# Linear attention and a gated FFN in one kernel: the order of work in the opening and in block 1

## The chip, the cores and the metric

The kernel runs on one core of one Trainium2 chip. The metric is device time in microseconds (us). The time before is the median of 11 runs. One more execution was recorded by the hardware profiler, and all durations of single instructions come from that one.

## What is computed

Inputs are q, k and v (batch 8, 8 heads, 576 positions, head dimension 64), the FFN's weights and a norm weight, all float32. The reference, cut to what matters:

```python
def phi(x, c, s):                       # c, s: cos and sin of the position
    r = np.maximum(x, 0.0)
    return np.concatenate([r * c, r * s], axis=-1)
q_p, k_p = phi(q, cos_w, sin_w), phi(k, cos_w, sin_w)
kv = np.einsum('bhsf,bhsd->bhfd', k_p, v)
z = np.sum(k_p, axis=2)
num = np.einsum('bhsf,bhfd->bhsd', q_p, kv)
den = np.einsum('bhsf,bhf->bhs', q_p, z)[..., None] + 1e-06
attn = num / den                        # then x = attn as (4608 tokens, 512)
rms = np.sqrt(np.mean(x * x, axis=-1, keepdims=True) + 1e-06)
xn = x / rms * rms_g
g = xn @ w_gate                         # 512 -> 1536
silu = g * (1.0 / (1.0 + np.exp(-g)))
out = (silu * (xn @ w_val)) @ w_out     # 1536 -> 512
```

## The kernel before

**Tiling.** Attention goes by batch. A batch has four chunks of 128 positions per head plus a tail of 64; two tails share a tile. The FFN goes by blocks of 512 tokens: block b holds the four chunks of batch b, and block 8 holds the tails of all eight. A block has 12 gval steps and then four out tiles (three and two halves for block 8). Gval step n computes 128 of the 1536 hidden columns for 512 tokens: four matmuls into a psG bank, four into a psV bank (gval_mm, L444), a Silu on ScalarE (ACT) out of psG (L453), and a multiply on VectorE (DVE) out of psV into hT (L459). An out tile is 12 matmuls of 512 columns into one bank (out_mm, L464), a copy to osb (out_store, L272 on ACT, L274 on DVE) and a store.

**Attention of a batch.** k_phi and q_phi make the feature map, one half on DVE (L215), one on ACT (L213). v_cast (L276) turns v to bf16 in two halves, LOW and HIGH (four heads each), v_cast_tail the tail on GpSimd. kvz_pe (L300) makes kv and z for eight heads, in psA, and kvz_evac copies them out. q is transposed, by DMA (q_tr_dma, L255) or, for batches 0 and 1, on TensorE (q_tr_pe, L263, and a copy, q_tr_evac). nd_pe (L328) makes numerator and denominator of a chunk in psA, nd_post (L378, L381, L382, DVE) divides, x_sq (L393, ACT) sums squares, GpSimd takes the power -0.5 (L398), x_norm (L405, DVE) scales, and x is transposed by DMA (x_tr_dma, L424) or on TensorE (x_tr_pe, L430, with a copy, x_tr_evac).

**Banks.** Of the eight PSUM banks psA has two, psG two, psV two. The last two are psO in the opening and psC, for the out tiles, afterwards. psA serves kvz, nd and some transposes in turn, so each waits until the one before has been read.

**Order.** The schedule is written out by hand: every engine works through its instructions in program order, and semaphores make it wait for data and for buffers to come free. Nothing is reordered by a planner.

- *Opening* (L488 to L626): batch 0's attention and, as its x chunks come, block 0's gval steps 0 to 5 in column pieces (open_ffn, L569, and open_h, L580 and L581) in three pairs of banks. Filler matmuls on a tile of zeros (L484) lie where TensorE would wait.
- *Block 0's steps 6 to 11*, with batch 1's phi work in between.
- *Out tiles of block 0* (L739 to L788): four tiles at once, in psC[0], psC[1], psG[0], psG[1], with batch 1's attention in between. At the end come four out_store, the first quarter of block 1's gval and the last x transposes of batch 1.
- *Blocks 1 to 8*: the loop at L808. A table of slots (at, L638; run, L641) hangs work of the next batch on a step: "pe" ahead of the step's matmuls, "pre" after the matmuls and ahead of Silu and multiply (or of out_store), "post" after them. Steps 12 to 15 are the out tiles. For batch 2 (`late`) all of it hangs on block 1: phi of k on steps 0 to 2, q on 2 to 4, v casts on 4 and 5, kvz on 6, nd on 7, 9, 11 and 12. For later batches k and v are done in the block before. (1,6) below means block 1, step 6.

**Queues.** Loads, stores and DMA transposes are issued from the SP queue, in program order; weights are issued from GpSimd's. The first slice of wo waits for k of batch 1, which waits for the third slice of w_gate. Batch 2 is loaded whole from L758 to L760; batch 3 in pieces of two heads hung on block 1's steps.

Of the kernel before, what the change touches and what calls it, by code (L numbers as in the profile page):

```python
# [22 lines left out]
def kernel(  # L23
# [18 lines left out]
    NNT = DFF // P  # L42
# [11 lines left out]
    psA = ps.tile([P, 2, 512], FP32, name="psA")  # L54
    psG = [ps.tile([P, 512], FP32, name=f"psG{i}") for i in range(2)]
    psV = [ps.tile([P, 512], FP32, name=f"psV{i}") for i in range(2)]
# [4 lines left out]
    psO = [ps_open.tile([P, 512], FP32, name=f"psO{i}") for i in range(2)]  # L61

    V, A, G = nc.vector, nc.scalar, nc.gpsimd
    LOW, HIGH = (0, 4), (4, 8)
# [143 lines left out]
    def view4(t, heads):  # L208
        return t[:, heads[0] : heads[1], :].rearrange("p h (j d) -> p h j d", d=D)

    def phi(eng, out_ap, in_ap, scale):
        if eng is nc.scalar:
            nc.scalar.activation(out=out_ap, in_=in_ap, func=AF.Relu, scale=scale)  # L213
        else:
            eng.tensor_scalar(  # L215
                out=out_ap, in0=in_ap, scalar1=scale, scalar2=0.0, op0=ALU.mult, op1=ALU.max
            )

    def k_phi(eng, b, c, part, heads=(0, 8)):

        o = slice(0, D) if part == 0 else slice(D, F)
        f = cos_of if part == 0 else sin_of
        if c < 4:
            if b not in kp_main:
                kp_main[b] = one.tile([P, 4, H, F], BF16, name="kpm", tag="kpm")
            src = view4(raw[("k", b)], heads)[:, :, c, :]
            phi(eng, kp_main[b][:, c, heads[0] : heads[1], o], src, f(c))
        else:
            phi(eng, kpt[b % 2][:, :, o], raw[("kt", b)][:, :, :], f(4))
# [35 lines left out]
    def q_tr_evac(eng, b, c, bank, heads=(0, 8)):  # L265
        h0, h1 = heads if c < 4 else (0, 4)
        dst = bank.bitcast(BF16).rearrange("p (h s) -> p h s", s=P)
        copy(eng, q_dst(b, c)[:, h0:h1, :], dst[:, h0:h1, :])
# [157 lines left out]
    def x_tr_pe(b, j, bank):  # L426
        xn = xn_of[(b, j)]
        dst = bank.bitcast(BF16).rearrange("p (t s) -> p t s", s=P)
        for t in range(NDT):
            nc.tensor.transpose(dst[:, t, :], xn[:, t * P : (t + 1) * P], ident[:, :])  # L430

    def x_tr_evac(eng, b, j, bank, part=(0, 4)):
        dst = bank.bitcast(BF16).rearrange("p (t s) -> p t s", s=P)
        copy(eng, x_dst(b, j)[:, part[0] : part[1], :], dst[:, part[0] : part[1], :])
# [5 lines left out]
    def gval_mm(blk, n, bank, cols=(0, TB), parts=((psG, wg), (psV, wv))):  # L440
        x = xnT[blk]
        for pst, w in parts:
            for t in range(NDT):
                nc.tensor.matmul(  # L444
                    pst[bank][:, cols[0] : cols[1]],
                    lhsT=w[:, t, n * P : (n + 1) * P],
                    rhs=x[:, t, cols[0] : cols[1]],
                    start=(t == 0), stop=(t == NDT - 1),
                )
# [13 lines left out]
    def out_mm(blk, j, n, bank):  # L463
        nc.tensor.matmul(  # L464
            bank, lhsT=hTs[blk][:, n, j * P : (j + 1) * P], rhs=wo[:, n, :],
            start=(n == 0), stop=(n == NNT - 1),
        )

    def out_store(eng, blk, j, bank):
        osb = four.tile([P, DM], FP32, name="osb", tag="osb")  # L470
        copy(eng, osb[:, :], bank)
        if blk < 8:
            rows = out[blk * S : blk * S + 512, :].rearrange("(p j) m -> p j m", j=4)
            nc.sync.dma_start(out=rows[:, j, :], in_=osb[:, :])  # L474
        else:
            for i in range(2):
                r0 = (2 * j + i) * S + 512
                nc.sync.dma_start(
                    out=out[r0 : r0 + 64, :], in_=osb[64 * i : 64 * i + 64, :]
                )  # L480

    def filler(n, bank):
        for _ in range(n):
            nc.tensor.matmul(bank, lhsT=warm[:, 0:P], rhs=warm[:, :], start=True, stop=True)  # L484
# [75 lines left out]
    def open_ffn(pair, steps, c0, c1, base=0, parts=(0, 1)):  # L560

        x = xnT[0]
        for i, n in enumerate(steps):
            for a in parts:
                w = (wg, wv)[a]
                bank = pairs[pair][a]
                lo = base + 256 * i + c0 % 256
                for t in range(NDT):
                    nc.tensor.matmul(  # L569
                        bank[:, lo : lo + c1 - c0],  # L570
                        lhsT=w[:, t, n * P : (n + 1) * P], rhs=x[:, t, c0:c1],
                        start=(t == 0), stop=(t == NDT - 1),
                    )
# [16 lines left out]
    q_tr_pe(0, 3, psO[1][:, :])  # L590
    x_norm(0, 1)
    open_ffn(0, (0, 1), 0, 128)
    x_tr_pe(0, 1, psA[:, 0, :])
    x_tr_evac(A, 0, 1, psA[:, 0, :])
    q_tr_evac(A, 0, 3, psO[1][:, :])
    nd_pe(0, 2, psA)
    nd_post(0, 2, psA)
    x_sq(0, 2)
    filler(1, psG[1][:, :])
    open_ffn(0, (0, 1), 128, 256)  # L600
    open_ffn(1, (2, 3), 0, 256, parts=(0,))
    nd_pe(0, 3, psA)
# [2 lines left out]
    open_ffn(2, (4, 5), 0, 256, parts=(0,))  # L605
    open_h(0, 0, 0)
    x_sq(0, 3)
    filler(2, psV[1][:, :])
    x_tr_pe(0, 2, psA[:, 0, :])
    x_tr_evac(A, 0, 2, psA[:, 0, :])  # L610
    open_ffn(1, (2, 3), 0, 256, parts=(1,))
    x_norm(0, 3)
    open_h(1, 2, 0)
    open_ffn(2, (4, 5), 0, 256, parts=(1,))
    x_tr_pe(0, 3, psA[:, 1, :])
    x_tr_evac(A, 0, 3, psA[:, 1, :])
    open_h(2, 4, 0)
    open_ffn(0, (0, 1), 256, 384)
    open_ffn(0, (0, 1), 384, 512)
    open_h(0, 0, 1)  # L620
    open_ffn(1, (2, 3), 256, 512)
# [9 lines left out]


    def none():
        return {"pe": [], "pre": [], "post": []}

    slots = {}

    def at(blk, n, where, f, *args):  # L638
        slots.setdefault((blk, n), none())[where].append((f, args))

    def run(blk, n, where):  # L641
        for f, args in slots.get((blk, n), none())[where]:
            f(*args)
# [25 lines left out]
    for nb in range(2, B):  # L669
        b = nb - 1  # L670
        late = nb == 2
        for c in range(5):
            kb, kn = (b, (c + 1) // 2) if late else (b - 1, 12 + (c * 3) // 5)
            at(kb, kn, "post", k_phi, V, nb, c, 0)
            at(kb, kn, "post", k_phi, A, nb, c, 1)
            qn = 2 + c // 2 if late else c
            at(b, qn, "post", q_phi, V, nb, c, 0)
            at(b, qn, "post", q_phi, A, nb, c, 1)
            at(b, qn, "post", q_tr_dma, nb, c)
        vb, vn = (b, 4) if late else (b - 1, 14)  # L680
        at(vb, vn, "post", v_cast, V, nb, LOW)
        at(vb, vn + 1, "post", v_cast, V, nb, HIGH)
        at(vb, vn, "post", v_cast_tail, G, nb)
        kz, nds = (6, (7, 9, 11, 12)) if late else (4, (5, 7, 9, 11))
        at(b, kz, "pe", kvz_pe, nb, psA)
        at(b, kz, "pre", kvz_evac, A, nb, psA, 0)
        at(b, kz, "pre", kvz_evac, A, nb, psA, 1)
        for j in range(4):
            n = nds[j]
            at(b, n, "pe", nd_pe, nb, j, psA)  # L690
            at(b, n, "pre", nd_post, nb, j, psA)
            at(b, n, "post", x_sq, nb, j)
            where = "pre" if n + 1 >= NNT else "post"
            at(b, n + 1, where, x_norm, nb, j)
            at(b, n + 1, where, x_tr_dma, nb, j)
        if nb % 2 == 1:
            at(b, 13, "pe", nd_pe, nb, 4, psA)
            at(b, 13, "pre", nd_post, nb, 4, psA)
            at(b, 13, "post", x_sq, nb, 4)
            at(b, 14, "post", x_norm, nb, 4)  # L700
            at(b, 14, "post", x_tr_dma, nb, 4)
    for nb in range(3, B):

        b = nb - 2
        for i, which in enumerate(("k", "v", "q")):
            for p in range(5):
                n = (0, 6, 10)[i] + p if b == 1 else 5 * i + p
# [11 lines left out]
    def out_step(blk, j):  # L719
        n = 12 + j  # L720
        run(blk, n, "pe")
        bank = psC[j % 2][:, :]
        for i in range(NNT):
            out_mm(blk, j, i, bank)
        run(blk, n, "pre")
        out_store(nc.scalar, blk, j, bank)
        run(blk, n, "post")
# [4 lines left out]
    banks0 = [psC[0][:, :], psC[1][:, :], psG[0][:, :], psG[1][:, :]]  # L732
# [7 lines left out]
    for n in range(NNT - 2):  # L740
# [25 lines left out]
        if n in nd_at:  # L766
            j = nd_at[n]
# [7 lines left out]
    for j in (2, 3):  # L775
        for n in (NNT - 2, NNT - 1):
            out_mm(0, j, n, banks0[j])
    out_store(A, 0, 2, banks0[2])
    out_store(V, 0, 3, banks0[3])
    for j in (0, 1):  # L780
        for n in (NNT - 2, NNT - 1):
            out_mm(0, j, n, banks0[j])
# [6 lines left out]
    x_tr_pe(1, 3, psC[1][:, :])  # L789
    x_tr_evac(V, 1, 3, psC[1][:, :])  # L790
    gval_mm(1, 1, 1, (0, 256), ((psV, wv),))
    for n in range(2):
        gval_mm(1, n, n, (256, 512))
        gval_h(1, n, n, gval_act(1, n, n))
# [21 lines left out]
    for half, bank in ((0, psC[1]), (1, psG[0])):  # L816
        c = slice(256 * half, 256 * half + 256)
# [41 lines left out]
```

## Time and profile before

| | us |
|---|---|
| median of 11 runs | 334.19 (333.96 to 335.89) |
| profiled execution, whole | 334.64 |
| its span, first to last instruction | 332.5 |
| TensorE matmuls (PE) busy | 320.8 (96%) |
| DVE busy | 181.4 (55%) |
| ACT busy | 169.2 (51%) |
| GpSimd (POOL) busy | 38.1 (11%) |
| granted TensorE clock | 1.00 |

A timeline line gives start and duration in us, the engine, the line of the kernel, the operation, what it writes and reads, and how many such instructions were merged; in brackets stand the idle time ahead of it and what ended that. PEld is the loading of weights into the array, which runs beside the matmuls. A line of waits gives the total time, the number of waits and the longest. Matmuls are pipelined and their ends are modelled.

### The profile page before, as it was taken

What the parts mean: (1) busy time and instruction counts of PE and PEld (TensorE: products, weight loads), DVE (VectorE), ACT (ScalarE), POOL (GpSimd) and SP (SyncE); (2) the same over time, 40 slices, a digit from 0 to 9 for tenths busy, and PEclk for the clock granted to TensorE, in tenths of its full rate; (3) what the DMA queues carried; (4) which work ended last, traced back from release to release, by engine and by line L of the source; (5) the groups of instructions that cost most, each with busy time, mean ns of one, the idle gap of its engine ahead of it and who ended that gap; (6) DMA issues with size and microseconds to landing.
All of it is one profiled execution on the core that took longest, in us unless ns stands there. A gap on an engine that the chain in (4) does not pass through costs nothing.

```text
span 332.5 us, 5954 instructions
## 1 busy us (share of the span) xinstructions
PE 320.8 (96%) x2191; PEld 163.7 (49%) x2191; DVE 181.4 (55%) x375; ACT 169.2 (51%) x327; POOL 38.1 (11%) x83
## 2 busy tenths in 40 slices
PE   8889999979899999999999999999999999999995
PEld 3568455635445544544454445444544444444443
DVE  3766576685755775567456765674567333204410
ACT  4564583675466546653665366545654233223321
POOL 3520221000120111012000110011001000000000
PEclk9999999999999999999999999999999999999999
DMA  8999997999688967786869886967531310020013
GB/s 208 276 187 242 310 203 188 321 266 178 161 236 191 194 172 219 180 205 148 240 141 221 161 240 157 220 157 237 126 72 39 106 55 0 2 100 26 0 34 96
DMA packets 95117, 54.14 MB, mean 163 GB/s; under 512 B 60016, under 2 KB 90480, under 8 KB 95088
## 3 DMA queue, kind: packets, MB, share of 16 engines
q1 hardware_dynamic: 89072, 48.65, 58.5%
q0 software_dynamic: 4768, 4.72, 8.8%
q10 hardware_dynamic: 1248, 0.39, 0.6%
q8 instruction: 17, 0.28, 0.3%
q14 instruction: 12, 0.10, 0.1%
HBM read 38.01 MB, written 9.44 MB: 143 GB/s over the span
## 4 chain that ended last, share of the span: by engine, by line
PE 87%; DVE 4%; DMA 4%; ACT 2%; issue 1%; SPq 1%; ACTq 0%; DVEq 0%
PE psC L464 25%; PE psG L444 25%; PE psV L444 25%; DMA rq<-in_q_dram 3%; PE psA L300 2%; PE psA L328 2%; DMA rk<-in_k_dram 1%; PE psG L569 1%; PE psV L569 1%; DVE xt L382 1%; PE psG L464 1%; DVE xn L405 1%; PE psO L569 1%; PE psG L484 1%; SPq L474 1%
## 5 line engine op out<-in xcount | busy, mean ns | idle before, releaser
L459 DVE TENSOR_TENSOR hT<-psV,sg 128x512 bf16<-128x512 f32 x102 | 70.3, 689 | 99.1 <-PE psV L444 87.9
L453 ACT ACTIVATE sg<-psG 128x512 f32<-128x512 f32 x102 | 60.6, 594 | 65.9 <-PE psG L444 65.7
L444 PE MATMUL psG<-xnT,wg 128*128 128x512 bf16 (+1 forms) x368 | 92.7, 374 | 0.4 <-ACT osb L272 0.3
L444 PE MATMUL psV<-xnT,wv 128*128 128x512 bf16 (+1 forms) x368 | 92.7, 374 | 0.0
L464 PE MATMUL psC<-wo,hT 128*128 128x512 bf16 x396 | 89.3, 379 | 0.0
L444 PEld LDWEIGHTS <-wv 128*128 128x128 bf16 x416 | 40.6, 98 | 47.4
L464 PEld LDWEIGHTS <-hT 128*128 128x128 bf16 x420 | 40.1, 98 | 46.7 <-DMA wo<-in_moe_w_out_dram 0.2
L444 PEld LDWEIGHTS <-wg 128*128 128x128 bf16 x416 | 38.5, 98 | 41.4 <-issue 1.2
L272 ACT COPY osb<-psC 128x512 f32<-128x512 f32 (+1 forms) x33 | 19.1, 580 | 45.3 <-PE psC L464 44.6
L398 POOL TENSOR_TENSOR rs<-ms,mhalf 128x1 f32<-128x1 f32 x36 | 19.9, 553 | 190.6 <-ACT scr L393 190.6
L405 DVE SCALAR_TENSOR_TENSOR xn<-xt,rs,gb 128x512 bf16<-128x512 f32 x36 | 27.3, 760 | 16.1 <-POOL rs L398 16.0
L393 ACT ACTIVATE scr<-xt 128x513 bf16<-128x513 f32 x36 | 22.9, 635 | 24.8 <-DVE xt L382 24.2
L382 DVE TENSOR_TENSOR xt<-psA,rec 128x512 f32<-128x512 f32 x35 | 24.2, 691 | 1.2
L213 ACT ACTIVATE qp<-rq,tab 128x512 bf16<-128x512 f32 x32 | 22.5, 714 | 1.1 <-DMA rq<-in_q_dram 1.1
L213 ACT ACTIVATE kpm<-rk,tab 128x512 bf16<-128x512 f32 (+1 forms) x34 | 21.2, 675 | 0.6 <-DMA rk<-in_k_dram 0.5
L215 DVE TENSOR_SCALAR kpm<-rk,tab 128x512 bf16<-128x512 f32 (+1 forms) x38 | 15.5, 460 | 4.3 <-ACT tab L168 3.3
L328 PEld LDWEIGHTS <-qpT 128*128 128x128 bf16 x248 | 11.9, 98 | 8.7 <-issue 2.5
L215 DVE TENSOR_SCALAR qp<-rq,tab 128x512 bf16<-128x512 f32 x32 | 15.1, 481 | 1.1 <-DMA rq<-in_q_dram 1.1
L484 PE MATMUL psG<-warm 128*128 128x512 bf16 x49 | 13.6, 421 | 1.2 <-DVE fidx L150 1.2
L328 PE MATMUL psA<-kvzs,qpT 128*128 128x65 bf16 x248 | 12.9, 193 | 1.7 <-DVE xt L382 0.9
L444 PE MATMUL psG<-xnt_tail,wg 128*128 128x512 bf16 x48 | 12.3, 379 | 0.0
L444 PE MATMUL psV<-xnt_tail,wv 128*128 128x512 bf16 x48 | 12.3, 379 | 0.0
(98 smaller groups left out, 195.4 us busy)
## 6 DMA issues: line engine op xcount, KB each, us to landing
out_dram<-osb SPq DMA_DIRECT2D x32, 256.0 KB, 2.7
rk<-in_k_dram SPq DMA_DIRECT2D x20, 256.0 KB, 3.3
rv<-in_v_dram SPq DMA_DIRECT2D x20, 256.0 KB, 3.3
rq<-in_q_dram SPq DMA_DIRECT2D x20, 256.0 KB, 3.6
rk<-in_k_dram SPq DMA_DIRECT2D x2, 1024.0 KB, 7.1
rq<-in_q_dram SPq DMA_DIRECT2D x2, 1024.0 KB, 9.3
rv<-in_v_dram SPq DMA_DIRECT2D x3, 512.0 KB, 10.2
wo<-in_moe_w_out_dram POOLq DMA_DIRECT2D x4, 384.0 KB, 8.7
```

Source lines behind the costliest of these rows:

```text
L213: nc.scalar.activation(out=out_ap, in_=in_ap, func=AF.Relu, scale=scale)
L215: eng.tensor_scalar(out=out_ap, in0=in_ap, scalar1=scale, scalar2=0.0, op0=ALU.mult, op1=ALU.max)
L272: nc.scalar.copy(out=o, in_=i)
L328: nc.tensor.matmul(o[:, g, i, :], lhsT=qpT[(b, 0)][:, h, j * P : (j + 1) * P], rhs=kvzs[(b, g)][:, i * E : (i + 1) * E], start=True, stop= ...
L382: nc.vector.tensor_tensor(out=xt[:, 0:DM].rearrange("p (b h d) -> p b h d", b=2, d=D), in0=o[:, :, :, 0:D], in1=rec[:, :, :].unsqueeze(3). ...
L393: nc.scalar.activation(out=scr[:, :], in_=xt[:, 0 : DM + 1], func=AF.Square, scale=1.0 / math.sqrt(DM), accum_out=ms[:, :],)
L398: nc.gpsimd.tensor_tensor(out=rs[:, :], in0=ms[:, :], in1=mhalf[:, :], op=ALU.pow)
L405: nc.vector.scalar_tensor_tensor(out=xn[:, :], in0=x_of[(b, j)][:, 0:DM], scalar=rs_of[(b, j)][:, :], in1=gb[:, :], op0=ALU.mult, op1=ALU. ...
L444: nc.tensor.matmul(pst[bank][:, cols[0] : cols[1]], lhsT=w[:, t, n * P : (n + 1) * P], rhs=x[:, t, cols[0] : cols[1]], start=(t == 0), sto ...
L453: nc.scalar.activation(out=sg[:, :], in_=psG[bank][:, :], func=AF.Silu)
L459: nc.vector.tensor_tensor(out=hTs[blk][:, n, :], in0=psV[bank][:, :], in1=sg[:, :], op=ALU.mult)
L464: nc.tensor.matmul(bank, lhsT=hTs[blk][:, n, j * P : (j + 1) * P], rhs=wo[:, n, :], start=(n == 0), stop=(n == NNT - 1),)
```

## The change

Nothing is computed differently. In the opening, the second x transpose of batch 0 goes to psV[1] instead of psA, the copy of the fourth transposed q chunk goes from ACT to DVE, one group of fillers grows from 1 to 2, one of 2 goes away, the ffn piece for columns 256 to 384 moves ahead of the fourth x transpose, and one filler follows that transpose. Among block 0's stores, DVE and ACT swap the tiles in psG[0] and psG[1]. Of batch 2's phi of k, two pieces on DVE and one on ACT are issued ahead of block 1's first Silu; the others move to steps 1 and 2. The LOW cast of v moves from step 4 to 3, ahead of the q work there, HIGH from 5 to 4, the tail cast from 4 to 3, and q chunks 1 to 4 move to steps 3, 5, 5 and 6, each with its DMA transpose. A new kind of slot, "mid", runs after half of an out tile's matmuls; only batch 2's last nd_pe, at (1,12), uses it.

```diff
     open_ffn(0, (0, 1), 0, 128)
-    x_tr_pe(0, 1, psA[:, 0, :])
-    x_tr_evac(A, 0, 1, psA[:, 0, :])
-    q_tr_evac(A, 0, 3, psO[1][:, :])
+    x_tr_pe(0, 1, psV[1][:, :])
+    x_tr_evac(A, 0, 1, psV[1][:, :])
+    q_tr_evac(V, 0, 3, psO[1][:, :])
     nd_pe(0, 2, psA)
     nd_post(0, 2, psA)
     x_sq(0, 2)
-    filler(1, psG[1][:, :])
+    filler(2, psG[1][:, :])
     open_ffn(0, (0, 1), 128, 256)
...
     x_sq(0, 3)
-    filler(2, psV[1][:, :])
     x_tr_pe(0, 2, psA[:, 0, :])
     x_tr_evac(A, 0, 2, psA[:, 0, :])
     open_ffn(1, (2, 3), 0, 256, parts=(1,))
     x_norm(0, 3)
     open_h(1, 2, 0)
     open_ffn(2, (4, 5), 0, 256, parts=(1,))
+    open_ffn(0, (0, 1), 256, 384)
     x_tr_pe(0, 3, psA[:, 1, :])
     x_tr_evac(A, 0, 3, psA[:, 1, :])
     open_h(2, 4, 0)
-    open_ffn(0, (0, 1), 256, 384)
+    filler(1, psA[:, 0, :])
     open_ffn(0, (0, 1), 384, 512)
...
     for nb in range(2, B):
         b = nb - 1
         late = nb == 2
+        vb, vn = (b, 3) if late else (b - 1, 14)
+        if late:
+            at(vb, vn, "post", v_cast, V, nb, LOW)
         for c in range(5):
-            kb, kn = (b, (c + 1) // 2) if late else (b - 1, 12 + (c * 3) // 5)
-            at(kb, kn, "post", k_phi, V, nb, c, 0)
-            at(kb, kn, "post", k_phi, A, nb, c, 1)
-            qn = 2 + c // 2 if late else c
+            kb, kn = (b, (1, 1, 1, 1, 2)[c]) if late else (b - 1, 12 + (c * 3) // 5)
+            if not late or c > 1:
+                at(kb, kn, "post", k_phi, V, nb, c, 0)
+            if not late or c > 0:
+                at(kb, kn, "post", k_phi, A, nb, c, 1)
+            qn = (2, 3, 5, 5, 6)[c] if late else c
...
-        vb, vn = (b, 4) if late else (b - 1, 14)
-        at(vb, vn, "post", v_cast, V, nb, LOW)
+        if not late:
+            at(vb, vn, "post", v_cast, V, nb, LOW)
         at(vb, vn + 1, "post", v_cast, V, nb, HIGH)
         at(vb, vn, "post", v_cast_tail, G, nb)
...
-            at(b, n, "pe", nd_pe, nb, j, psA)
+            at(b, n, "mid" if n == NNT else "pe", nd_pe, nb, j, psA)
...
         for i in range(NNT):
+            if i == NNT // 2:
+                run(blk, n, "mid")
             out_mm(blk, j, i, bank)
...
-    out_store(A, 0, 2, banks0[2])
-    out_store(V, 0, 3, banks0[3])
+    out_store(V, 0, 2, banks0[2])
+    out_store(A, 0, 3, banks0[3])
...
     gval_mm(1, 1, 1, (0, 256), ((psV, wv),))
+    k_phi(V, 2, 0, 0)
+    k_phi(V, 2, 1, 0)
+    k_phi(A, 2, 0, 1)
     for n in range(2):
         gval_mm(1, n, n, (256, 512))
         gval_h(1, n, n, gval_act(1, n, n))
```

More of the change, by code (lines that the diff above doesn't have):

```diff
@@ L633, in none @@
     def none():
-        return {"pe": [], "pre": [], "post": []}
+        return {"pe": [], "mid": [], "pre": [], "post": []}
     slots = {}
```

## The prediction

> **What bounds the kernel now.** I read the busy table first, then TensorE's waits, then the timelines of the stretches where those waits lie. The first line is from the page's busy table; the next five are the waits of PE (total, times, longest, in us).
>
> ```profile
> PE 320.8 (96%) x2191; PEld 163.7 (49%) x2191; DVE 181.4 (55%) x375; ACT 169.2 (51%) x327; POOL 38.1 (11%) x83
> ```
> ```profile
> PE psA L300 <- DVE vvm L274: 1.8, 2, 1.4
> ...
> PE psA L328 <- DVE xt L382: 0.9, 1, 0.9
> PE psA L328 <- ACT xnT L272: 0.7, 1, 0.7
> ...
> PE psG L444 <- ACT osb L272: 0.3, 1, 0.3
> ```
> PE sets the time; no other engine passes 55%. So a change is worth only what it takes out of PE's gaps, and all the long ones lie before 88 us: the chain after 98 us is PE work back to back. Now the gaps, in PE's timeline. A group of four 512-column matmuls takes 0.865 us from start to start (75.16 to 76.03); I measure gaps from start to start, because the listed idle leaves out about 0.15 us of drain.
>
> ```profile
> 68.94 1.03 PE L444 MATMUL psV<-xnT,wv 128*128 128x512 bf16 x4
> 70.07 1.02 PE L444 MATMUL psG<-xnT,wg 128*128 128x512 bf16 x4
> 70.93 1.03 PE L444 MATMUL psV<-xnT,wv 128*128 128x512 bf16 x4
> 73.36 0.28 PE L300 MATMUL psA<-vvm,kpm 128*128 128x65 bf16 x4 [1.41 <-DVE vvm L274]
> ...
> 74.56 0.28 PE L300 MATMUL psA<-vvm,kpm 128*128 128x65 bf16 x4 [0.44 <-DVE vvm L274]
> ...
> 85.42 1.03 PE L444 MATMUL psV<-xnT,wv 128*128 128x512 bf16 x4
> 87.31 0.41 PE L328 MATMUL psA<-kvzs,qpT 128*128 128x65 bf16 x8 [0.87 <-DVE xt L382]
> ```
> Block 1 loses 70.07-69.80 = 0.27, 73.36-71.80 = 1.56, 74.56-73.96 = 0.60 and 87.31-86.28 = 1.03: 3.46 us. The 1.56 and 0.60 end on DVE's two v casts, which DVE reaches late:
>
> ```profile
> 72.36 0.34 DVE L215 TENSOR_SCALAR qp<-rqt,tab 128x256 bf16<-128x256 f32 x1
> 72.62 0.69 DVE L274 CAST vvm<-rv 128x1024 bf16<-128x1024 f32 x1
> 73.22 0.68 DVE L459 TENSOR_TENSOR hT<-psV,sg 128x512 bf16<-128x512 f32 x1
> 73.82 0.68 DVE L274 CAST vvm<-rv 128x1024 bf16<-128x1024 f32 x1
> ```
> The opening has one gap that the change touches (nd_pe(0,2) after an evacuation from psA), and a wall behind it:
>
> ```profile
> 20.78 0.39 PE L430 MATMUL psA<-ident,xn 128*128 128x128 bf16 x4
> 21.84 0.41 PE L328 MATMUL psA<-kvzs,qpT 128*128 128x65 bf16 x8 [0.67 <-ACT xnT L272]
> ```
> ```profile
> 45.31 0.55 PEld L464 LDWEIGHTS <-hT 128*128 128x128 bf16 x4 [0.21 <-DMA wo<-in_moe_w_out_dram]
> ```
> The first slice of wo is issued at 36.84 and takes 8.4 us: it lands at 45.24. Its issue waits for k of batch 1, itself behind the weights, all DMA. So PE cannot begin the out matmuls of block 0 before 45.3, whatever the opening does; today it gets there at 45.10.
>
> **Part 1, the opening.** With its own bank, nd_pe(0,2) goes straight after the x transpose (21.00, not 21.84). What is late next is the first ffn piece, which needs the same evacuation: an x transpose takes 1.06 us from start to its reader (20.78 to 21.84), so that piece starts at 21.84, not 22.31: 0.47 saved, two fillers (0.43) inside the wait. The q copy on DVE (0.68, against 1.01 on ACT at 21.68) fits between x_norm(0,1), over at 20.42, and nd_post(0,2), at 21.45: free, and without that cover at most 0.68. nd_pe(0,3) follows at 23.60 (before 24.07), and x_tr_pe(0,2) still starts 2.3 us later, since its x_norm stands behind nd_post(0,3) on DVE: 25.90. The two fillers removed ahead of it only become idle time. Then the move: before, x_tr_pe(0,3) at 28.36 was covered by ffn columns 256-384 (0.89) until columns 384-512 at 29.47. Now those 0.89 us come first (27.87 to 28.76), the transpose starts at 28.76, and columns 384-512 can start only at 28.76+1.06 = 29.82; a filler covers 0.22 of it. Its x_norm(0,3) would have been ready at about 27.4 anyway. So PE is 0.35 us later than before (+0.84 -0.47, with rounding), and reaches the wall at 45.45: +0.14. Bounds: 0 (any gain dies at the wall) to +0.35 (nothing absorbed).
>
> A rule of the Trainium skill speaks against idle in place of fillers: "TensorE: Matmul & The Clock Gate", "A second HAM failure mode: psum-queue depth-cycling", says that short idles between matmul groups while cycling PSUM banks can send the clock to half and back. The row: after the 1.41 us idle at 73.36 the next 512-column groups still take 0.865, and the granted clock is 1.00 in every stretch. The new idle at 24.7 is about 1.2 us. By the row: 0. By the rule, one window of 3.4 us (the same page, Part 1) at half rate costs an estimated 1.7 us. I take the row.
>
> **Part 2, stores of block 0.** gval_mm(1,0) needs psG[0] empty. Before, ACT copied it at 59.79 behind an x evacuation, and PE resumed at 60.43. Now DVE takes it right after x_norm(1,2), near 59.17, done at 59.86 (0.69); PE runs on when its out matmuls end, 60.00. Gain 0.43, of which x_norm(1,3) on DVE (over at 61.55, while the transpose before was at 61.96) leaves 0.39. ACT's copy of psG[1] at 59.79-60.38 is early enough for 61.1.
>
> **Part 3, batch 2 ahead.** Two k_phi on DVE (0.40 each) and one on ACT (0.65) go ahead of block 1's first hT and Silu. The idle there is 1.33 us on DVE (62.81 to 64.15) and 0.72 on ACT; k of batch 2, issued at 52.17, took 6.3, so it is there at 58.5. Free; without the cover, 0.85 on DVE. No DMA moves with them. Then I replay both queues, 0.25 us early from parts 1 and 2:
> - ACT: three k_phi to 66.4, Silu of step 2 at 66.3, q chunk 0 and the k tail (1.1 us, before 2.3), Silu 3 by 68.4. PE needs its bank at 69.56, so the 0.27 goes.
> - DVE: hT 3 at 68.4, LOW cast at 69.0 (v, issued at 58.00, took 9.1: landed at 67.1), q chunk 1 0.40, hT 4 at 70.1, HIGH cast 70.7 to 71.3. Queued behind the LOW cast's wait would be all of those, but the load is 1.9 us early.
> - PE comes to kvz at 71.29; its second four heads, 0.6 later, need HIGH by 71.9: 0.6 spare. The 1.56 and 0.60 go. The tail casts on GpSimd were at 67.41 to 68.3, early enough.
>
> q chunks 2 and 3 move from step 3 to step 5, with their transposes on SP: ready at 72.9, behind the k loads of batch 3 issued by 73.4, two issues of 1.25 to 75.8, landing in 3.6 to 4.6, so by 80. nd_pe(2,2) comes at 81.7 (84.30 before). Chunk 1 lands near 74 for 77.9.
>
> **Part 4, the last nd.** nd_pe(2,3) waited 1.03 us for nd_post(2,2) to leave psA, 87.26-84.30 = 2.96 after nd_pe(2,2). New: psA is free at 81.66+2.96 = 84.62, the out tile begins at 83.64, and after six of its matmuls (6 x 0.216) the nd comes at 84.94, so there is no wait, by 0.3. Without that half tile, 1.0 would stand. The x transpose of batch 2 that comes out of it was issued at 93.30 and landed by 96.1, 2.3 ahead of block 2; its chain now comes 3.0 earlier and block 2 3.7, so 1.5 stay.
>
> **Sum.** +0.14 -0.39 -3.46 = -3.71. The profiled execution took 334.64 (span 332.5 and 2.1 around it), so 330.93; it lies 0.45 above the runs' median of 334.19, so I put the median at 330.5.
>
> **The rivals.**
> - *A new wait in block 1* (0.18). The margins on HIGH (0.6) and the last nd (0.3) are small. If ACT's Silus slip by two phi (1.3 us), HIGH ends at 72.5, kvz waits 0.6 and the last nd another 0.6: 331.7. For it: before, DVE and ACT were both behind here. Against: ACT loses 1.2 us of work in step 2.
> - *The clock gate*, as priced: 330.5+1.7 = 332.2 (0.03).
> - *The v load blocks DVE* (slower). The LOW cast now stands ahead of q chunk 1, hT 4 and HIGH in an in-order queue. If v landed as slowly as the slowest weight load (16.1 us: at 74.1), HIGH would end at 74.1+0.60+0.40+0.61+0.60 = 76.3, kvz 1.8 later than before; the nd's 1.03 is kept: 334.2+0.8 = 335.0. It decides from a landing at 73.3 on, 6.2 us later than seen. Against: the change puts no new transfer ahead of v. Slower 0.06, within 0.2% (landing near 73, or the new order not taking effect) 0.03.
>
> **The numbers.** The forecast gets 0.70, from 330.0 (opening free, no wait anywhere) to 331.0. To hold 8 in 10 the range takes in the new wait: 330.0 to 332.0. Faster 0.91, same 0.03, slower 0.06; 0.2%, 0.7 us, is about what this measurement can tell from none.
>
> **What would show it.** Right: nd_pe(0,2) directly behind its transpose, yet about 0.6 us idle after the filler ahead of columns 384-512, and out matmuls of block 0 still starting at 45.3 to 45.5; gval of block 1 at 60.1 without a wait; kvz of batch 2 in one piece at 71.3; nd_pe(2,3) between out matmuls with no idle; block 2 at about 94.7 (98.41). Wrong: a wait of kvz on vvm, of PE on a Silu in steps 2 to 6, or of nd on qpT; 512-column groups longer than 0.865; v landing after 69.

## The result and the profile after

The changed kernel takes 332.53 us (median of 12 runs, 332.10 to 333.54) against 334.12 for the kernel before: a ratio of 0.9944, 95% interval 0.9931 to 0.9956. That is 1.6 us faster. The ratios here and below compare means, and some executions of the kernel before, 7 of these 47, lie at 335.6 to 336.0, some 1.6 above the rest, so versions are best compared by their medians. The prediction said 330.5, at most 332.0: it had the direction, and it promised 2.0 us too much. The profiled execution took 333.54 (span 331.4), 1.1 less than that of before.

PE is busy for 321.2 us, as before (320.8). Two of its waits are new (total, times, longest).

```profile
PE psG L444 <- DMA xnT<-xn: 2.4, 1, 2.4
...
PE psA L484 <- ACT xnT L272: 0.7, 1, 0.7
```
The waits on vvm, on xt and on osb are gone, and so is that of nd_pe on the x evacuation; but a filler (L484) now waits 0.7 for such an evacuation in the opening (more on it under e6 to e8). The longest wait of all is one that the kernel before did not have: a gval matmul waits for a DMA transpose of x. PE's timeline after shows where:

```profile
60.16 0.60 PE L444 MATMUL psG<-xnT,wg 128*128 128x256 bf16 x4
...
71.35 0.28 PE L300 MATMUL psA<-vvm,kpm 128*128 128x65 bf16 x4
...
72.55 1.03 PE L444 MATMUL psG<-xnT,wg 128*128 128x512 bf16 x4
...
83.68 1.46 PE L464 MATMUL psC<-wo,hT 128*128 128x512 bf16 x6
84.97 0.42 PE L328 MATMUL psA<-kvzs,qpT 128*128 128x65 bf16 x8
85.23 4.05 PE L464 MATMUL psC<-wo,hT 128*128 128x512 bf16 x18
...
89.58 5.35 PE L464 MATMUL psC<-wo,hT 128*128 128x512 bf16 x24
97.31 1.02 PE L444 MATMUL psG<-xnT,wg 128*128 128x512 bf16 x4 [2.37 <-DMA xnT<-xn]
```
Block 1's gval starts at 60.16 without a wait (predicted 60.1), kvz of batch 2 runs in one piece at 71.35 (71.3), the last nd lies inside its out tile at 84.97 (84.94) with no idle, and the out tiles end at 89.58 + 24 x 0.2162 = 94.77 (94.7). Up to here PE is 98.41 - 94.77 = 3.64 us ahead, close to the 3.71 of the prediction (0.22 of it is not the change's doing, as shown further below). Then PE stands until 97.31, and 2.54 of it is lost.

What it waits for is the fourth x chunk of batch 2. First SP's queue after, then that of before, over the same work; each line is an issue and how long it held the queue.

```profile
86.02 1.28 SPq L85 DMA_DIRECT2D rvt<-in_v_dram  x2
87.34 2.21 SPq L74 DMA_DIRECT2D rq<-in_q_dram  x2
89.65 1.23 SPq L424 DMA_TRANSPOSE xnT<-xn  x1
90.99 0.52 SPq L474 DMA_DIRECT2D out_dram<-osb  x1
91.56 0.42 SPq L74 DMA_DIRECT2D rq<-in_q_dram  x1
92.08 1.28 SPq L424 DMA_TRANSPOSE xnT<-xn  x1
```
```profile
90.29 1.82 SPq L424 DMA_TRANSPOSE xnT<-xn  x1
...
93.30 1.20 SPq L424 DMA_TRANSPOSE xnT<-xn  x1
```
And the landing of that one transpose (last column: us from issue to landing), after and then before:

```profile
xnT<-xn SPq DMA_TRANSPOSE x1, 5.1
```
```profile
xnT<-xn SPq DMA_TRANSPOSE x1, 4.9
```
Before, it was issued at 93.30 and landed at 98.2, 0.2 us ahead of block 2 at 98.41: it was just hidden. After, its input is ready at 90.20 (the end of x_norm on DVE), but SP issues it only at 92.08, behind the third transpose, a store and a q load; the third transpose, ready at 86.91, had itself been held to 89.65 by two v tail loads and two q loads. The fourth lands at 97.17.

### The profile page after: what moved, and what is told of

Its sections match the earlier page's. It is cut to its first block, busy times and chain, and to the rows that moved or that the text cites. A ratio compares the mean times of both kernels' runs of the same rounds, so it can differ in the third digit from the quotient of the medians.

```text
span 331.4 us, 5951 instructions
## 1 busy us (share of the span) xinstructions
PE 321.2 (97%) x2191; PEld 163.9 (49%) x2191; DVE 182.0 (55%) x376; ACT 168.5 (51%) x326; POOL 38.1 (11%) x83
## 4 chain that ended last, share of the span: by engine, by line
PE 86%; DVE 5%; DMA 4%; issue 2%; ACT 2%; POOL 0%; SPq 0%; ACTq 0%; DVEq 0%
PE psG L444 25%; PE psV L444 25%; PE psC L464 23%; PE psA L300 3%; DMA rq<-in_q_dram 2%; PE psA L328 2%; DMA xnT<-xn 2%; PE psG L464 1%; DVE xt L382 1%; PE psG L569 1%; DVE xn L405 1%; PE psV L569 1%; PE psO L569 1%; PE psG L484 1%; ACT scr L393 1%
## 5 line engine op out<-in xcount | busy, mean ns | idle before, releaser
L484 PE MATMUL psG<-warm 128*128 128x512 bf16 x50 | 14.9, 446 | 1.2 <-DVE fidx L150 1.2
```

## The experiments

**The fourth x chunk on TensorE (e1).** The transpose is taken off the DMA path.

```diff
-            at(b, n + 1, where, x_tr_dma, nb, j)
+            if late and j == 3:
+                at(b, 14, "mid", x_tr_pe, nb, j, psV[1][:, :])
+                at(b, 14, "mid", x_tr_evac, V, nb, j, psV[1][:, :])
+            else:
+                at(b, n + 1, where, x_tr_dma, nb, j)
```


> The changed kernel, with batch 2's fourth x chunk transposed on TensorE in half of out tile (1,14) into psV[1] and copied by DVE, instead of by the DMA transpose that landed at 97.17. Theory (all gains of the change arrive at 94.8, and only this one landing holds block 2): the gap of 2.54 us from 94.77 to 97.31 goes, four transposes cost 0.22: 332.5 - 2.3 = 330.2. Rival (the DMA engines or SP's queue as a whole are late, so the next transfer holds block 2, the third x chunk or q of batch 3): a wait of 1 us or more stays at the head of block 2: 331.5 to 332.5.

Measured: 330.78, ratio 0.9882 (0.9859 to 0.9905). The four transposes lie at 91.03 and block 2 follows its out tile without a wait:

```profile
91.03 0.39 PE L430 MATMUL psV<-ident,xn 128*128 128x128 bf16 x4
91.25 4.05 PE L464 MATMUL psC<-wo,hT 128*128 128x512 bf16 x18
95.14 1.03 PE L444 MATMUL psG<-xnT,wg 128*128 128x512 bf16 x4
```
This one landing held block 2, and nothing waits behind it. The total is 0.6 above the 330.2 expected, because I had taken the 2.54 of the profiled execution off the median time. The median execution has a gap of 1.63 (e12 below), and 332.53 - 1.63 + 0.22 = 331.1. The 0.3 that is left lies outside the span: with this transpose on TensorE (e1, e5, e7, e8, e9) every run takes 1.7 to 1.9 more than its span, in the kernel before and the changed one 2.1 to 2.2. Why is open.

**q loads from another queue (e2).** Batch 3's four main q loads are issued by GpSimd. (Cut from the diff: load_piece gets the queue as an argument.)

```diff
...
-                at(b, n, "post", load_piece, which, nb, p)
+                pool = b == 1 and which == "q" and p < 4
+                at(b, n, "post", load_piece, which, nb, p, nc.gpsimd if pool else nc.sync)
```


> The changed kernel, with the four main q loads of batch 3 issued from GpSimd's queue instead of SP's, so that SP has less ahead of the x transposes. Theory that SP's issuing is late: the third x transpose is issued near 87 (89.65 now), the fourth near 90.3 (92.08 now), and block 2 starts 1.8 us sooner: 330.8. Rival, that the DMA engines are full (busy share 1.02 from 85 to 94.8) and the issue time hardly matters: the fourth is issued at 90.3 and lands no sooner than 96.5: 332.0 to 332.5.

Measured: 332.80, ratio 0.9946 (0.9927 to 0.9966): no better. The transpose went out 1.9 us sooner, and took 5.7 instead of 5.1, landing at 95.88; block 2 started at 95.96 in this execution (332.36). The eight runs lie in two groups, 332.2 to 332.5 and 333.1 to 333.4; their mean granted clock is 0.998 to 1.000 in both, and what parts them is open. So an earlier issue alone does not make it: the landing grows. The Trainium skill ("DMA: Bandwidth & Descriptors", "Issuing engines are not separate DMA queues") says the same, that issuing from another engine saves only the sequencer's time.

**No q loads (e10), and q loads after the transpose (e11).** In e10 they are skipped (`continue`); in e11 the first three move to step 13.

```diff
                 n = (0, 6, 10)[i] + p if b == 1 else 5 * i + p
+                if b == 1 and which == "q" and p < 3:
+                    n = 13
```


> The changed kernel, with the four main loads of q of batch 3 (1 MB) left out; its q chunks 0 to 3 are made from batch 2's q, so batch 3's rows are not the reference's. Theory (the fourth x transpose of batch 2 lands late because of the q traffic around it: it waits for SP to issue them, and then shares the DMA engines with them): it is issued near 90.3, lands within 3.5 us, by 93.8, and block 2 starts without a wait: 330.3. Rival (a DMA transpose at this place takes 5 us whatever else moves): issued at 90.3, it lands at 95.3, and 0.5 of wait is left: 330.8 to 331.0. If SP and q have nothing to do with it: 332.5.

> The changed kernel, with the first three main q loads of batch 3 issued after the fourth x transpose of batch 2 instead of ahead of it; nothing is left out. Theory (the transposes go out near 87.0 and 90.3 and find free DMA engines): landing by 94, block 2 without a wait, and q, landing near 97, is a little late for its first use at (2,0), which PE does not feel: 330.5. Rival 1 (a transpose takes 5 us anyway): 331. Rival 2 (q is now so late that ACT, waiting for it, holds up the next Silu and PE): a wait on a Silu in block 2's first steps, 331.5 or more.

Measured: e10 330.94, ratio 0.9876 (0.9848 to 0.9903); e11 331.92, ratio 0.9905 (0.9880 to 0.9930). The issue of the transpose in e10 (in e11 it is at 90.27), and its landing, which is the same in both:

```profile
90.20 1.20 SPq L424 DMA_TRANSPOSE xnT<-xn  x1
```
```profile
xnT<-xn SPq DMA_TRANSPOSE x1, 2.4
```
Without the q traffic around it the same transpose takes 2.4 us, not 5, and block 2 starts at 94.75 and 94.81, without a wait. The time of e10 alone would have fitted the rival's 330.8 to 331.0, since the theory's 330.3 again took the profiled gap off the median; it is the landing of 2.4 that rules the rival out. That settles the cause: q loads of batch 3, in SP's queue and in the DMA engines, with the engines' mean busy share from 85 to 94.8 at 1.02 in the changed kernel, 0.60 in e10 and 0.66 in e11 (the profile's measure can pass 1). In e11 rival 2 came true: ACT stands 2.91 us for q, and PE meets a wait on a Silu (0.49 us idle) in block 2's fourth step. The median is about 1 us above that of e10; the profiled execution, 331.65, shows only part of it.

**The last nd, in four surroundings (e3, e4, e5).** e3 (the changed kernel) and e5 (e1) put "pe" back for "mid" with the edit below; e4 gives the kernel before only the "mid" slot.

```diff
-            at(b, n, "mid" if n == NNT else "pe", nd_pe, nb, j, psA)
+            at(b, n, "pe", nd_pe, nb, j, psA)
```


> The changed kernel, with batch 2's last nd_pe back ahead of out tile (1,12) instead of in its middle. Theory (block 2 starts when the x transpose lands, so what PE wins ahead of it is given back): PE waits about 1.0 us at 83.7 for psA, the wait at the head of block 2 shrinks by as much, and the time is the same or 0.2 better, since the nd itself is no later: 332.3 to 332.5. Rival (the half-tile placement is worth its 1.0 us): 333.5.

> The kernel before, with only the last nd_pe of batch 2 moved into the middle of its out tile. The prediction's step (the x transpose has 2.3 us to spare ahead of block 2): the 1.03 us wait at 87.31 goes and the time falls by 1.0, to 333.1. Theory now (in the kernel before the transpose issued at 93.30 took 4.9 and landed at 98.2, 0.2 ahead of block 2): at most 0.2 is won, 333.9 to 334.2, and a wait of about 0.8 to 1.0 appears at the head of block 2.

> The kernel with the fourth x chunk of batch 2 on TensorE (330.8), with batch 2's last nd_pe back ahead of its out tile. Theory (the half-tile placement is worth its 1.0 us as soon as no DMA transpose stands behind it): 331.8, with PE waiting about 1.0 for psA at 83.8. Rival (it was worth nothing in the changed kernel and stays so): 330.8.

Measured: e3 332.75, ratio 0.9941 (0.9919 to 0.9962), the same as the changed kernel; e5 331.78, ratio 0.9911 (0.9886 to 0.9936), 1.00 slower than e1; e4 333.65, ratio 0.9978 (0.9958 to 0.9998). e3 shows the exchange in two waits:

```profile
PE psA L328 <- DVE xt L382: 0.9, 1, 0.9
PE psG L444 <- DMA xnT<-xn: 0.7, 1, 0.7
```
The 0.9 us are back, and the wait on the transpose is 0.7 instead of 2.4. So the half-tile placement is worth 1.0 us where no transpose stands behind it and nothing in the changed kernel, where one does. In e4 my theory's size was off: the transpose took 4.3 us in that profile, not 4.9, and about 0.6 of the 1.03 arrived (the kernel before had a median of 334.30 beside it).

**The kernel before, with the fourth chunk on TensorE (e9).** The edit is that of e1, with the "mid" slot that it needs.

> The kernel before, with only the fourth x chunk of batch 2 transposed on TensorE. Theory (there the DMA transpose landed 0.2 us ahead of its use and held nothing): no gain, 0.2 us of added transposes: 334.3 to 334.6. Rival (a DMA transpose costs the kernel time in itself, apart from its landing): 332 or so, as in the changed kernel.

Measured: 334.82, ratio 1.0005 (0.9984 to 1.0025). The median says little here: it falls between six runs at a mean granted clock of 0.999 or 1.000 (333.8 to 334.3) and six at 0.995 (335.4 to 335.9); the last section comes back to these. No difference, as expected: before, the transpose held nothing. Its loss is the change's own doing, by bringing PE forward.

**The opening (e6, e7, e8).** e6 is the changed kernel, e7 is e1, each with the first part of this edit; e8 adds the second part to e7.

```diff
-    open_ffn(0, (0, 1), 256, 384)
     x_tr_pe(0, 3, psA[:, 1, :])
     x_tr_evac(A, 0, 3, psA[:, 1, :])
     open_h(2, 4, 0)
-    filler(1, psA[:, 0, :])
+    open_ffn(0, (0, 1), 256, 384)
...
-    tc.add_manual_dep(w.ins, d.ins.name, SYNC_DEP, reason="after k of batch 1")
+    tc.add_manual_dep(w.ins, weight_dmas[4].ins.name, SYNC_DEP, reason="after the weights")
```


> The changed kernel, with columns 256 to 384 of the first ffn piece back behind the fourth x transpose and without the filler there, and the DMA transpose of batch 2 as in the changed kernel. Theory (the 0.84 us of the opening arrive wherever wo has landed early enough, since all of block 1, its x transposes too, goes with PE): 331.7 to 331.9. Rival (the landing of the x transpose is set by DMA traffic that does not move with PE): 332.5.

> The kernel with the fourth x chunk on TensorE (330.8), with columns 256 to 384 of the first ffn piece back behind the fourth x transpose and without the filler there. Theory of the prediction (0.84 us saved in the opening, all but 0.15 to 0.4 of it lost again waiting for the first slice of wo near 45.2): 330.4 to 330.65, with a wait on wo ahead of the first out matmul. Rival (the landing of wo is no wall, what the opening saves arrives): 329.95.

> As the run with the opening's order put back, and in addition the first slice of wo waits for the third slice of w_gate instead of for k of batch 1, so that it lands some 7 us sooner and k, q and v of batch 1 later by up to 1.6 us (384 KB more ahead of them). Theory (wo was the wall, v of batch 1 has some tenths to spare): out matmuls begin near 44.7 and 0.3 to 0.7 more is won: 329.8 to 330.2. Rival (the loads of batch 1 become the wall, kvz at 49 waits for v or its tail): 330.6 or slower.

Measured: e6 331.84, ratio 0.9916 (0.9883 to 0.9948); e7 329.92, ratio 0.9858 (0.9832 to 0.9885); e8 329.69, ratio 0.9848 (0.9820 to 0.9877). e6 came out as expected, 0.69 below the changed kernel. In e7 my theory fell: 0.86 less than e1, where I had expected at most 0.4. Nor is 0.84 what the edit saves. From the start of batch 0's first x transpose, ahead of which all versions do the same, to the start of the first out matmul, the profiles show:

| | us |
|---|---|
| order before, no wait for wo (e4, e9) | 26.20 |
| order before, with its wait for wo (before) | 26.40 |
| changed order (eight profiles) | 26.78 to 26.79 |
| e6 and e8, no wait for wo | 25.74, 25.73 |
| e7, with a wait for wo | 26.75 |

So the changed order costs 0.58 against the order before and 1.05 against that of e6 to e8. What the prediction had wrong is the new filler. It was to cover 0.22 of PE's wait for the fourth x transpose; in the changed kernel it waits for the copy of that transpose itself:

```profile
28.56 0.39 PE L430 MATMUL psA<-ident,xn 128*128 128x128 bf16 x4
29.62 0.38 PE L484 MATMUL psA<-warm 128*128 128x512 bf16 x1 [0.67 <-ACT xnT L272]
29.84 0.38 PE L569 MATMUL psG<-xnT,wg 128*128 128x128 bf16 x4
```
The transpose writes half 1 of psA, the filler half 0; why the filler waits for the reading of the other half, the trace does not say. Columns 384 to 512 could have started at 29.62 and start at 29.84: the filler adds 0.22 and hides nothing. 0.84 + 0.22 makes the 1.05. (In e6 only 0.69 of it arrived; its profile has a gap of about 2.4 at the head of block 2, so part may have gone there.)

The wall, the landing of wo that PE cannot pass, is real all the same. The profiled execution of e7 (330.73, the slowest of five) shows it:

```profile
45.37 0.61 PE L464 MATMUL psC<-wo,hT 128*128 128x512 bf16 x2 [0.86 <-DMA wo<-in_moe_w_out_dram]
```
In the thirteen profiles that leave its order alone, the first slice of wo is issued anywhere from 35.4 to 36.9 and takes 8.2 to 8.5, so it lands between 43.8 and 45.3. In e7's profile it is issued at 36.89, and PE, which without the wait would be there at 18.62 + 25.73 = 44.35, begins 1.02 later. The other four executions took 329.56 to 330.19, 0.6 to 1.2 less than e1, so there more than half of the 1.05 arrived. In e8 the slice is issued at 28.21, the out matmuls begin at 44.24, and all four runs lie between 329.59 and 329.77: 1.09 below e1, all of the 1.05, without e7's spread. e8 is the fastest version tried, 2.8 us below the changed kernel.

**The changed kernel again (e12).**

> The changed kernel once more, unaltered, for a second look at the landing of batch 2's fourth x transpose: its first profiled execution (333.54) lies 1.0 above its median (332.53). Theory (the landing varies with DMA traffic, and the first profile caught a late one): the gap at the head of block 2 is between 1 and 2 us here, the transpose takes 3.5 to 4.5 and the execution 332.1 to 333.0. Rival (the gap is 2.5 in every execution and the 1.0 lies elsewhere): again about 2.5.

Measured: 332.56, ratio 0.9935 (0.9911 to 0.9962); the profiled execution took 332.57.

```profile
89.54 5.35 PE L464 MATMUL psC<-wo,hT 128*128 128x512 bf16 x24
96.36 1.02 PE L444 MATMUL psG<-xnT,wg 128*128 128x512 bf16 x4 [1.47 <-DMA xnT<-xn]
```
This is a median execution: the transpose, issued at 91.95, took 4.3, and the gap is 96.36 - 94.73 = 1.63.

## Why the prediction was wrong, point by point

**The step that failed** is the last of part 4: "The x transpose of batch 2 that comes out of it was issued at 93.30 and landed by 96.1, 2.3 ahead of block 2; its chain now comes 3.0 earlier and block 2 3.7, so 1.5 stay." I took the landing time from the table of DMA issues, where it is the median of all x transposes, and most of those lie in quieter stretches:

```profile
xnT<-xn SPq DMA_TRANSPOSE x24, 2.8
```
The transpose in question took 4.9, and its slack was 0.2. The term that failed is thus the landing that this slack rests on, together with an issue that was taken to move with its chain. Worked out again with the numbers of the profile after: issued at 92.08 instead of about 90.3 (1.8, SP's queue) and 5.1 instead of 2.8 (2.3), together 4.1, less the 1.5 to 1.6 that I had, gives 2.5; measured, 2.54 (1.63 in e12, issued at 91.95 and 4.3 to land). Both terms go back to batch 3's q loads (e10, e11). I had named the margin, but priced no case in which it failed.

**A second term, smaller:** part 1's "a filler covers 0.22 of it". The filler stood behind the wait, not in it, and the opening lost 0.58 instead of 0.35. The sign that the prediction named, 0.6 us idle after the filler, came as 0.67 ahead of it.

**Right, with its size:** parts 2 and 3, and the nd of part 4. The replayed queues of DVE and ACT put kvz at 71.29 and 71.35 was measured. None of the three rivals came in the profile after: no wait on a Silu, a clock of 1.00 from 60 to 94.8, and v landed near 66. The 1.0 of the last nd is real (e5 against e1) but was given back at block 2 (e3).

**Right by luck:** the out matmuls at 45.45 (measured 45.47). Two errors cancel. The opening took 26.78, where 26.40 + 0.14 = 26.54 was forecast, but this execution came to the first x transpose sooner than that of the kernel before, with nothing changed ahead of it; the first two lines are from the profile after, the last is from that of before:

```profile
18.69 0.40 PE L430 MATMUL psG<-ident,xn 128*128 128x128 bf16 x4
...
45.47 0.59 PE L464 MATMUL psC<-wo,hT 128*128 128x512 bf16 x2
```
```profile
18.91 0.40 PE L430 MATMUL psG<-ident,xn 128*128 128x128 bf16 x4
```
Counted from there, PE comes to the head of block 2 after 76.08 instead of 79.50 us: the change has won 3.42 by then, not 3.64. "Whatever the opening does" was wrong too: wo landed late in the one profile that I had, and in the profile of the changed kernel (issued at 35.41, 8.4 to land) no wall stood in the way. The bound "nothing absorbed" was the better choice, and still 0.2 too low.

**The sum again,** for the median: 330.5 predicted; + 0.24 to 0.44 for the opening (0.38 or 0.58, as the kernel before does or does not wait for wo, instead of 0.14); + 1.6 for the gap at block 2 (e12). That makes 332.3 to 332.5, against 332.53 measured.

## What to carry to other kernels

A wait taken out of the busiest engine is won only if everything due later is early enough: for each such transfer, look up its own issue and its own landing, not the median of its kind, and check whether it is only just hidden. In this kernel one transfer took twice as long in a busy stretch as in a quiet one, and moving the loads ahead of it to another queue, so that it went out sooner, did not help while the same traffic surrounded it. A filler helps only if it does not wait itself: look up its own wait. A landing time seen in one profile is one draw; before it serves as a wall, look at it in a second.

## What the runs showed that was not expected

The clock can fall after an idle of PE of little more than 2 us. In the profile of e6 PE stood idle 2.26 us at the head of block 2, and the matmuls after it ran at half rate; the columns of the window rows are busy time and count of PE, PEld, DVE, ACT and POOL, granted clock, DMA share and GB/s.

```profile
96.09 1.81 PE L444 MATMUL psG<-xnT,wg 128*128 128x512 bf16 x4 [2.26 <-DMA xnT<-xn]
...
99.40 1.13 PE L444 MATMUL psG<-xnT,wg 128*128 128x512 bf16 x4 [0.22 <-issue]
```
```profile
93.80:96.10 2.30, 0.04 (x2) 0.04 (x2) 0.56 (x1) 0.58 (x1) 0.00 (x0) 1.00 1.06 269
96.10:99.60 3.50, 3.28 (x8) 1.30 (x10) 0.00 (x0) 1.21 (x2) 0.00 (x0) 0.51 0.88 239
```
The granted clock is 0.51 for 3.5 us. Two groups took 99.40 - 96.09 = 3.31 instead of 1.73, so about 1.6 us are lost, and that execution took 334.51 where four of the other five took 331.2 to 332.1. After the idle of 2.37 us in the changed kernel's profile the clock stayed at 1.00, and likewise after the 1.2 us or so of new idle in the opening. The Trainium skill ("TensorE: Matmul & The Clock Gate", "Part 1") has the clock fall after an idle window of about 3.4 us, and the window run free of the kernel; here 2.26 us were enough. That the window runs free could be why 2.37 us did no harm in another execution, but no run here tests it.

The kernel before meets such a fall more often than its one profile, at 1.00 throughout, showed when I took the row over the rule. The mean granted clock of every execution timed beside the experiments is known. In 20 of 64 of the kernel before, and in 8 of 24 of e4 and e9, which keep all or most of its waits in block 1, it was 0.994 or 0.995, and these took 1.6 to 2.0 us more than the others (medians); of the changed kernel and its variants 2 of 75 were so low, e6's profiled execution being one. Half a per cent of 334 us is an estimated 1.7 us, the size of the loss in e6's profile. So the change also took away most of these falls, a gain that the prediction did not count and the medians hardly show. Which idle brings them about in the kernel before is open, since none of those executions was profiled.
